# A subtraction on GpSimd cut into pieces of 256 columns, in an attention and two-layer MLP kernel

## The chip, the cores and the metric

The kernel runs on one core of a Trainium2 chip. The metric is the device time of one execution in microseconds. TensorE is called PE here, VectorE DVE, ScalarE ACT, GpSimd POOL, and SyncE SP, as in the profile.

## The reference

Three parts follow one another; the output of each is the input of the next.

1. Attention over 4 batches, 8 heads, 576 positions, head size 64. Scores are scaled by 1/8; those more than tau = 0.02 below their row's maximum are left out; softmax; product with v. The result is laid out as 2304 tokens of 512 numbers.
2. An MLP, 512 to 2048 to 512, with a rational activation between: `g = P(h) / (Q(h) + 1e-6)`, P of third and Q of second degree in h and |h|.
3. A second MLP of the same sizes with a piecewise quadratic activation: h where h >= 1, 0 where h <= -1, (h + 1)^2 / 4 between.

Inputs and outputs are float32, the four weight matrices float64. The kernel keeps close to float32 accuracy with float16 matrix products: each operand is the sum of an upper half, `hi` (its value rounded to float16), and a lower half, `lo` (what the rounding left out, again in float16). A product is made of hi x hi, hi x lo and lo x hi.

## The kernel before

**Making the halves.** ACT casts the float32 value to float16 (`hi`), then `lo = src - hi` is computed by DVE or by POOL. The function `split` (L188 to L200) does this for most operands. With no scale it is ACT's cast (L191) and POOL's subtraction (L192); with a scale and `on_vector` it is ACT's scaling (L194) and one operation on DVE (L195); with a scale and without `on_vector`, ACT scales in place (L197) and `split` calls itself with no scale, so that POOL subtracts.

**Weights.** Each layer has 8 chunks with two halves each (`x` = 0 for the first matrix, 1 for the second), a half being 128 x 1024 numbers (E = 1024). `convert` loads a half from DRAM on SP's queue (L221), turns float64 into float32 by three DVE operations on integers (L208 to L210), finds a bound (ACT's L226 and a small PE product, L170), and calls `split` without `on_vector`: so the subtraction of a weight is a POOL instruction of 1024 columns at L192, 16 times into `wc` for the first layer and 16 times into `wh` for the second. The other things that come to L192 are `gg`, the activations of the MLP steps (384 columns, 192 times), and for the first batch `qk` (576) and `v` (512). The halves go out to DRAM and are loaded again for later batches.

**Attention.** For each batch and pair of heads, q and k are loaded, split and transposed by DMA. Then come nine rows of 128 queries against 576 keys (36 rows a batch, 144 in all). Each row runs: scores on PE (L357, L358); maximum on DVE (L407 for the first batch; L410 for the others, where it also copies the scores to SBUF); two small operations (L411 on ACT, L412 on DVE); exponential on ACT (L367); the threshold applied on DVE, `e = (s >= th) * e` (L368); the cast to float16 on ACT (L376); the lower half on POOL in two instructions, the 64 columns of the last block (L377) and the other 512 columns (L378); the transpose of both halves by DMA, issued on SP's queue (L380); the product with v on PE (L393); and the normalizing on DVE, PE and ACT (L430 to L444). Three rows' `hl` and `eT` buffers exist (N_ROW = 3).

**MLP.** Tokens go through in 12 blocks of 192 for each layer, and each block in 8 steps, one for each chunk. A step makes the first product on PE (L641), the activation on ACT and DVE (L526 to L535 for the first layer, L586 to L588 for the second; L529, L530 and L588 read the product in PSUM, L528, L533, L534, L535 and L587 read SBUF alone), the halves `gg` (ACT's L191, POOL's L192), and the second product (L655). The second product of a step is issued three steps later (LAG = 3).

**Order.** The work of the first batch's attention and the first layer's weights comes first. Then run the 192 MLP steps, and beside them the second layer's weights (spread over steps 0 to 20) and the attention of the following batches (`ATTENTION`, spread over steps 18 to 147). Each group of instructions gets a due time by `at(...)`, and the planner of the language orders each engine's instructions by those times, the dependences and its own estimates. On the chip every engine runs its instructions strictly in that order; SP's queue issues almost all DMAs, in order too.

Of the kernel before, what the change touches and what calls it, by code (L numbers as in the profile page):

```python
# [12 lines left out]
ALU = mybir.AluOpType  # L13
# [23 lines left out]
def tile_attention_moe_moe2(  # L37
# [18 lines left out]
    V, A, G, T, Q = nc.vector, nc.scalar, nc.gpsimd, nc.tensor, nc.sync  # L56
    B, H, S, D = q.shape
    P = 128
# [14 lines left out]
    E = KT * CF  # L73
# [114 lines left out]
    def split(hi, lo, src, scale=None, on_vector=True):  # L188

        if scale is None:  # L190
            A.copy(hi, src)  # L191
            G.tensor_tensor(lo, src, hi, op=ALU.subtract)  # L192
        elif on_vector:
            A.activation(hi, src, AF.Copy, scale=scale)  # L194
            V.scalar_tensor_tensor(lo, src, scale, hi, op0=ALU.mult, op1=ALU.subtract)  # L195
        else:
            A.activation(src, src, AF.Copy, scale=scale)  # L197
            split(hi, lo, src)
# [14 lines left out]
    def convert(m, i, x, dst, on_vector):  # L213

        if x == 0:
            raw = rp.tile([P, KT, CF * words], raw_type, name=f"rw{m}_{i}_0", tag="rw")
            src = w_in_dram[m][:, i * CF * words : (i + 1) * CF * words].rearrange("(kt p) f -> p kt f", p=P)
        else:
            raw = rp.tile([P, NF, DM * words], raw_type, name=f"rw{m}_{i}_1", tag="rw")
            src = w_out_dram[m][i * CF : (i + 1) * CF, :].rearrange("(f p) d -> p f d", p=P)  # L220
        Q.dma_start(raw, src)  # L221
        name = f"{m}_{i}_{x}"
        src = as_float(raw.rearrange("p a b -> p (a b)"), name)
        hi, lo = dst[:, 0:E], dst[:, E : 2 * E]
        bound = small(1, "mb" + name)
        A.activation(hi, src, AF.Square, scale=2.0**-32, accum_out=bound)  # L226
        s = root("pw" + name, f_w[m][x][:, i : i + 1], everywhere("mw" + name, bound, 1), even=m == 1 and x == 1)
        split(hi, lo, src, s, on_vector)
        if m == 0 and x == 0:

            pg = ps_1.tile([P, 512], F32, name="pg" + name, tag="aux")[:, 0:CF]
            cols = hi.rearrange("p (kt f) -> p kt f", kt=KT)
            for f in range(NF):
                c = slice(f * P, (f + 1) * P)
                for kt in range(KT):
                    T.matmul(pg[:, c], cols[:, kt, c], cols[:, kt, c], start=(kt == 0), stop=(kt == KT - 1))
            V.tensor_reduce(gram[:, i : i + 1], pg, axis=AX.X, op=ALU.max)
        elif i == NCH - 1:
            f_max[m][x] = small(1, f"f_max{m}{x}", True)
            V.tensor_reduce(f_max[m][x], f_w[m][x], axis=AX.X, op=ALU.max)  # L240
# [29 lines left out]
    def prep_v(b, on_vector):  # L270
# [24 lines left out]
        for g, raw in enumerate(raws):  # L295
            n = H if g == H // hs else hs * NT
            for n0 in range(0, n, 8):
                n1 = min(n, n0 + 8)
                to = vv[:, g * hs * NT + n0 : g * hs * NT + n1]
                split(to[:, :, 0:D], to[:, :, D + 1 : 2 * D + 1], raw[:, n0:n1], s_x[b], on_vector)  # L300
        return vv

    def prep_pair(b, pr, on_vector):
# [23 lines left out]
        for x in range(2):  # L327
            split(qk[:, x, :, 0:D], qk[:, x, :, D : 2 * D], raw[:, x], s[:, x : x + 1], on_vector)
# [12 lines left out]
    M = NT * P  # L341
# [19 lines left out]
    def softmax(b, s, ab, con, nb, th, name):  # L361

        if b == 0:
            e = mp.tile([P, 2 * W], F32, name="e" + name, tag="tp", bufs=N_TEMP)[:, 0:S]
        else:
            e = ap.tile([P, S], F32, name="e" + name, tag="e", bufs=N_SC)
        A.activation(e, s, AF.Exp, bias=nb, scale=con[:, 0:1])  # L367
        V.scalar_tensor_tensor(e, s, th, e, op0=ALU.is_ge, op1=ALU.mult)  # L368
        hl = ap.tile([P, 2 * S], F16, name="hl" + name, tag="hl", bufs=N_ROW)
        if ab == 0:  # L370

            hi, whole, half, lo_w, lo_h = hl[:, 0:S], slice(0, M), slice(M, S), hl[:, S + ST :], hl[:, S : S + ST]
        else:

            hi, whole, half, lo_w, lo_h = hl[:, S:], slice(ST, S), slice(0, ST), hl[:, 0:M], hl[:, M:S]
        A.copy(hi, e)  # L376
        G.tensor_tensor(lo_h, e[:, half], hi[:, half], op=ALU.subtract)  # L377
        G.tensor_tensor(lo_w, e[:, whole], hi[:, whole], op=ALU.subtract)  # L378
        eT = ap.tile([P, C, P], F16, name="eT" + name, tag="eT", bufs=N_ROW)
        Q.dma_start_transpose(out=eT, in_=hl)  # L380
        return eT
# [13 lines left out]
    def att_rows(b, pr, g, data, pvs):  # L395

        con, qkT, kT2, vv, h = data
        name = f"{b}_{pr}_{g}"
        rows = ROWS[3 * g : 3 * g + 3]
        for r, (t, ab) in enumerate(rows):  # L400
            other = b == 0 and r % 2 == 1
            banks = ps_2.tile([P, 1024], F32, name=f"s{name}_{r}", tag="acc" if other else "s")
            scores(banks, t, ab, qkT, kT2)
            mx, nt = small(1, f"mx{name}_{r}"), small(2, f"nt{name}_{r}")
            if b == 0:
                s = banks[:, 0:S]
                V.tensor_reduce(mx, s, axis=AX.X, op=ALU.max)  # L407
            else:
                s = ap.tile([P, S], F32, name=f"sc{name}_{r}", tag="sc", bufs=N_SC)
                V.tensor_scalar(s, banks[:, 0:S], 1.0, -LARGEST, op0=ALU.mult, op1=ALU.max, accum_out=mx)  # L410
            A.activation(nt[:, 1:2], mx, AF.Identity, bias=ln_e, scale=con[:, 1:2])  # L411
            V.tensor_scalar(nt[:, 0:1], mx, con[:, 2:3], None, op0=ALU.add)  # L412
            eT = softmax(b, s, ab, con, nt[:, 1:2], nt[:, 0:1], f"{name}_{r}")
            if ab == 0:
                pv = ps_1.tile([P, 512], F32, name=f"pv{b}_{pr}_{t}", tag="ph" if b == 0 else "pv", bufs=2 if b == 0 else 1)
                pvs[t] = pv[:, 0 : 2 * (2 * D + 2)].rearrange("p (a d) -> p a d", a=2)
            if t < NT:
                weighted(pvs[t][:, ab], slice(0, P), eT, slice(0, P), vv, h + ab, ab)
            else:
                for i in range(2):  # L420
                    c = slice(i * ST, (i + 1) * ST)
                    weighted(pvs[t][:, 0], c, eT, c, vv, h + i, 0)
            if ab == 1 or t == NT:
                normalize(b, pr, t, pvs.pop(t))
# [331 lines left out]
```

## Time and profile before

| | |
|---|---|
| three runs | 1320.09, 1316.28, 1324.3 us; median 1320.09 |
| the profiled execution | 1324.86 us; its span from the first to the last instruction 1323.1 us |
| mean granted TensorE clock | 0.916 of full speed |
| busy: PE, DVE, ACT, POOL | 1056.3, 1050.1, 839.3, 515.6 us |

Engines: the busy time of each is a mean over stages that differ much, so a table by stretches stands first among the rows below. In a list of a line's instructions, a duration that is far above the median, on an engine that runs in order, is time in which the instruction was issued and could not go on. In the timeline a row is an instruction: its start, its duration, its engine and line.

### The profile page before, as it was taken

How to read it: one execution, taken by the hardware profiler on the slowest of the kernel's cores; microseconds unless marked ns; L12 is line 12 of the kernel's file. 1: busy time of each engine (PE TensorE's matmuls, PEld its weight loads, DVE VectorE, ACT ScalarE, POOL GpSimd, SP SyncE). 2: the span in 40 equal slices, each digit the busy share in tenths (PEclk: the TensorE clock that was granted, in tenths of full speed). 3: DMA queues.
4: the chain of work that ended last, by engine and by line, in shares of the span. 5: the costliest groups of instructions: out<-in, count | busy, mean ns of one | idle time of the engine just before them, and what ended most of it. 6: DMA issues, size and time to landing. Idle time of an engine off the chain costs nothing.

```text
span 1323.1 us, 31559 instructions
## 1 busy us (share of the span) xinstructions
PE 1056.3 (80%) x12498; PEld 961.1 (73%) x12498; DVE 1050.1 (79%) x2461; ACT 839.3 (63%) x1515; POOL 515.6 (39%) x541
## 2 busy tenths in 40 slices
PE   1455555677754899889888999999889998999998
PEld 1233334577743888789777888898778898999998
DVE  6777776899979999678999776779998777897421
ACT  3767764677754676667676576767765776776332
POOL 2656563344332555432145354321354453222221
PEclk9985556799976999899999999999999999999999
DMA  6778875433566666781278465922586549205100
GB/s 211 221 204 225 204 190 176 147 113 112 195 258 202 119 118 108 162 243 29 73 185 201 95 121 105 242 62 46 134 216 132 94 80 258 79 2 192 65 14 26
DMA packets 260277, 187.14 MB, mean 141 GB/s; under 512 B 220960, under 2 KB 233248, under 8 KB 251936
## 3 DMA queue, kind: packets, MB, share of 16 engines
q1 hardware_dynamic: 260128, 185.12, 54.9%
q8 instruction: 98, 1.61, 0.5%
q14 instruction: 51, 0.42, 0.1%
HBM read 106.96 MB, written 21.50 MB: 97 GB/s over the span
## 4 chain that ended last, share of the span: by engine, by line
DVE 31%; PE 26%; DMA 12%; issue 11%; ACT 8%; POOL 7%; SPq 2%; DVEq 0%; POOLq 0%; ACTq 0%
PE acc L655 12%; PE ph L641 11%; DMA eT<-hl 7%; DVE e L368 4%; POOL hl L378 3%; DVE wt L209 2%; DMA qkT<-qk 2%; DVE sc L410 2%; DMA rqk<-in_k_dram 2%; DVE t L534 2%; DVE t L535 2%; PE pv L393 2%; DVE t L533 2%; DVE t L587 2%; POOL gg L192 2%
## 5 line engine op out<-in xcount | busy, mean ns | idle before, releaser
L655 PE MATMUL acc<-gg,wc 128*128 128x192 f16 x4608 | 428.4, 248 | 12.4 <-POOL gg L192 6.3
L641 PEld LDWEIGHTS <-wc 128*128 128x128 f16 x4608 | 393.8, 100 | 47.0 <-DVE t L530 29.3
L655 PEld LDWEIGHTS <-wc 128*128 128x128 f16 x4608 | 385.6, 99 | 13.4 <-issue 11.8
L192 POOL TENSOR_TENSOR gg<-t,gg 128x384 f16<-128x384 f32 x192 | 197.9, 1031 | 476.1 <-ACT gg L191 382.3
L641 PE MATMUL ph<-xT,wc 128*128 128x192 f16 x2304 | 221.9, 255 | 34.5 <-DVE t L530 32.4
L641 PE MATMUL ph<-yT,wc 128*128 128x192 f16 x2304 | 219.5, 248 | 1.2 <-DVE t L588 0.9
L378 POOL TENSOR_TENSOR hl<-e,hl 128x512 f16<-128x512 f32 x144 | 173.5, 1205 | 0.0
L393 PE MATMUL pv<-v,eT 128*128 128x65 f16 (+1 forms) x2240 | 105.8, 206 | 67.2 <-DMA eT<-hl 58.7
L393 PEld LDWEIGHTS <-eT 128*128 128x128 f16 (+1 forms) x2240 | 94.1, 109 | 84.0 <-DMA eT<-hl 71.4
L191 ACT CAST gg<-t 128x384 f16<-128x384 f32 x192 | 97.1, 507 | 87.6 <-DVE t L588 43.8
L377 POOL TENSOR_TENSOR hl<-e,hl 128x64 f16<-128x64 f32 x144 | 62.4, 433 | 198.8 <-ACT hl L376 198.4
L357 PE MATMUL s<-qkT 128*128 128x512 f16 (+2 forms) x320 | 94.8, 326 | 45.6 <-DVE e L368 17.8
L376 ACT CAST hl<-e 128x576 f16<-128x576 f32 x144 | 96.2, 668 | 53.6 <-DVE e L368 43.7
L587 DVE SCALAR_TENSOR_TENSOR t<-t,c 128x384 f32<-128x384 f32 x96 | 71.6, 746 | 67.9 <-ACT t L586 67.8
L368 DVE SCALAR_TENSOR_TENSOR e<-sc,nt,e 128x576 f32<-128x576 f32 x108 | 97.4, 902 | 29.2 <-ACT e L367 28.9
L586 ACT ACTIVATE t<-ph,c 128x384 f32<-128x384 f32 x96 | 63.9, 666 | 56.7 <-PE ph L641 51.2
L367 ACT ACTIVATE e<-sc,nt,con 128x576 f32<-128x576 f32 x108 | 93.5, 866 | 6.6 <-POOL hl L378 0.2
L526 ACT ACTIVATE t<-ph,sc 128x384 f32<-128x384 f32 x96 | 55.1, 574 | 60.2 <-PE ph L641 59.9
L411 ACT ACTIVATE nt<-mx,ln_e,con 128x1 f32<-128x1 f32 x144 | 55.2, 384 | 55.1 <-DVE sc L410 44.7
L410 DVE TENSOR_SCALAR_CACHE_REDUCE sc<-s 128x576 f32<-128x576 f32 x108 | 80.9, 749 | 10.8 <-PE s L358 10.4
L531 ACT ACTIVATE t<-t,lc 128x384 f32<-128x384 f32 x96 | 67.9, 707 | 31.4 <-DVE t L528 31.1
L358 PE MATMUL s<-kT,qkT 128*128 128x512 f16 (+2 forms) x320 | 76.5, 324 | 2.8 <-DMA kT<-qkT 2.8
(172 smaller groups left out, 1646.2 us busy)
## 6 DMA issues: line engine op xcount, KB each, us to landing
wc<-scratch SPq DMA_DIRECT2D x56, 1024.0 KB, 6.0
rw<-in_moe_w_in_dram SPq DMA_DIRECT2D x16, 1024.0 KB, 5.5
rw<-in_moe_w_out_dram SPq DMA_DIRECT2D x16, 1024.0 KB, 5.6
scratch<-wc SPq DMA_DIRECT2D x8, 1024.0 KB, 4.3
scratch<-wh SPq DMA_DIRECT2D x16, 512.0 KB, 2.6
kT<-qkT SPq DMA_DIRECT2D x32, 144.0 KB, 2.6
rqk<-in_q_dram SPq DMA_DIRECT2D x16, 256.0 KB, 3.1
rqk<-in_k_dram SPq DMA_DIRECT2D x16, 256.0 KB, 3.0
```

The costliest lines, as they stand in the source:

```text
L191: A.copy(hi, src)
L192: G.tensor_tensor(lo, src, hi, op=ALU.subtract)
L357: T.matmul(s[rows, at : at + w], qkT[:, c, cols], k1[:, k0 : k0 + w], start=True, stop=False)
L367: A.activation(e, s, AF.Exp, bias=nb, scale=con[:, 0:1])
L368: V.scalar_tensor_tensor(e, s, th, e, op0=ALU.is_ge, op1=ALU.mult)
L376: A.copy(hi, e)
L378: G.tensor_tensor(lo_w, e[:, whole], hi[:, whole], op=ALU.subtract)
L393: T.matmul(pv[rows, 0:w], eT[:, c, cols], vv[:, h * NT + x if x < NT else H * NT + h, at : at + w], start=(n == 0), stop=(n == len(blocks) ...
L410: V.tensor_scalar(s, banks[:, 0:S], 1.0, -LARGEST, op0=ALU.mult, op1=ALU.max, accum_out=mx)
L587: V.scalar_tensor_tensor(u, u, top, u, op0=ALU.min, op1=ALU.mult)
L641: last = T.matmul(ph[:, f, :], w[:, wx, kt, f * P : (f + 1) * P], rhs, start=(n == 0), stop=(n == 3 * KT - 1))
L655: T.matmul(dst, w[:, wx, f, d * P : (d + 1) * P], gg[:, gx, f, :], start=(i == 0 and f == 0 and n == 0 and d % 2 == 0), stop=(i == NCH - 1 ...
```

## The change

Two places at which POOL makes a lower half are cut along the columns. In `split` without a scale, a source of 128 x 1024 (a weight's half) is subtracted in four instructions of 256 columns in place of one of 1024; other shapes stay one instruction. In `softmax`, the 512 columns of a row are subtracted in two instructions of 256; the one of 64 columns ahead of them stays. The pieces are written one after the other; values and buffers are the same.

```diff
         if scale is None:
             A.copy(hi, src)
-            G.tensor_tensor(lo, src, hi, op=ALU.subtract)
+
+            n = E // 4 if tuple(src.shape) == (P, E) else None
+            for p in [slice(c, c + n) for c in range(0, E, n)] if n else [slice(None)]:
+                G.tensor_tensor(lo[:, p], src[:, p], hi[:, p], op=ALU.subtract)
...
         G.tensor_tensor(lo_h, e[:, half], hi[:, half], op=ALU.subtract)
-        G.tensor_tensor(lo_w, e[:, whole], hi[:, whole], op=ALU.subtract)
+        for p in (slice(0, M // 2), slice(M // 2, M)):
+            G.tensor_tensor(lo_w[:, p], e[:, whole][:, p], hi[:, whole][:, p], op=ALU.subtract)
```

## Rows read from the trace of the kernel before

**Rows 1.** Busy time by stretches: us of the stretch, then each engine's.

```profile
0.00:240.00 240.00, 111.19 (x908) 73.29 (x909) 177.14 (x418) 149.73 (x260) 118.77 (x115) 0.72 0.75 204
240.00:420.00 180.00, 117.93 (x1204) 110.15 (x1204) 165.52 (x328) 117.68 (x196) 67.11 (x41) 0.84 0.48 166
420.00:1130.00 710.00, 640.80 (x8156) 592.47 (x8154) 595.94 (x1481) 474.21 (x888) 288.57 (x342) 0.98 0.61 136
1130.00:1323.00 193.00, 186.41 (x2236) 185.14 (x2233) 111.44 (x236) 97.67 (x175) 41.13 (x45) 0.99 0.17 59
```

**Rows 2.** The chain that ended last: by engine; by line, whole span; 0 to 240 us.

```profile
DVE 31%; PE 26%; DMA 12%; issue 11%; ACT 8%; POOL 7%; SPq 2%; DVEq 0%; POOLq 0%; ACTq 0%
...
by line: PE acc L655 11.7%; PE ph L641 11.1%; issue 10.8%; DMA eT<-hl 6.9%; DVE e L368 3.7%; POOL hl L378 3.0%; DVE wt L209 2.4%; DMA qkT<-qk 2.2%; DVE sc L410 2.0%; DMA rqk<-in_k_dram 1.9%; DVE t L534 1.8%; DVE t L535 1.8%; PE pv L393 1.8%
...
by line: issue 13.1%; DVE wt L209 6.5%; DMA eT<-hl 6.2%; POOL hl L378 5.9%; POOL wc L192 4.9%; DVE wt L210 4.4%; ACT wt L197 3.2%; DVE e L368 3.2%; DVE wt L208 2.7%; POOL hl L377 2.5%; DMA rqk<-in_k_dram 2.4%; PE pv L393 2.2%; ACT wc L191 2
```

**Rows 3.** Instructions of DVE lines: shortest/median/longest ns, first and last start us.

```profile
L535 DVE SCALAR_TENSOR_TENSOR t<-t,t x96: 537/554/2479, 247.6 to 1213.7; 128x384 f32<-128x384 f32 x96
...
L208 DVE TENSOR_SCALAR wt<-rw x32: 678/693/2607, 8.9 to 399.1; 128x1024 int32<-128x1024 int32 x32
...
L588 DVE SCALAR_TENSOR_TENSOR t<-ph,c,t x96: 597/617/619, 416.7 to 1307.8; 128x384 f32<-128x384 f32 x96
```

**Rows 4.** Timeline: the first and last waits behind an L378, then behind a weight.

```profile
45.39 1.03 DVE L323 SCALAR_TENSOR_TENSOR con<-qkf,cflag 128x1 f32<-128x1 f32 x1
...
1117.96 1.51 DVE L534 SCALAR_TENSOR_TENSOR t<-t,qc 128x384 f32<-128x384 f32 x1
...
24.76 2.61 DVE L208 TENSOR_SCALAR wt<-rw 128x1024 int32<-128x1024 int32 x1
...
409.60 2.12 POOL L192 TENSOR_TENSOR wh<-wt,wh 128x1024 f16<-128x1024 f32 x1 [1.52 <-issue]
409.83 2.50 DVE L195 SCALAR_TENSOR_TENSOR qk<-rqk,qk_s,qk 128x576 f16<-128x576 f32 x1
```

**Rows 5.** The chain in order of time: first and last piece with such a wait.

```profile
45.47 0.95 DVE con L323
...
1082.38 0.89 DVE t L587
```

**Rows 6.** Instructions of POOL's lines, and who waited for L192 (us, times).

```profile
L377 POOL TENSOR_TENSOR hl<-e,hl x144: 296/306/1282, 44.5 to 1117.3; 128x64 f16<-128x64 f32 x144
...
L378 POOL TENSOR_TENSOR hl<-e,hl x144: 1145/1156/1672, 44.8 to 1117.6; 128x512 f16<-128x512 f32 x144
...
L192 POOL TENSOR_TENSOR gg<-t,gg x192: 907/916/2884, 248.8 to 1309.1; 128x384 f16<-128x384 f32 x192
...
L192 POOL TENSOR_TENSOR wc<-wt,wc x16: 2120/2124/3099, 23.7 to 227.7; 128x1024 f16<-128x1024 f32 x16
...
L192 POOL TENSOR_TENSOR v<-rv,v x5: 1117/1117/1119, 36.1 to 40.4; 128x512 f16<-128x512 f32 x5
...
  POOL gg L192: 50.5, 19
  PE acc L655: 6.3, 8
```

**Rows 7.** Timeline from 59.9 us: POOL and DVE.

```profile
59.97 1.15 POOL L378 TENSOR_TENSOR hl<-e,hl 128x512 f16<-128x512 f32 x1
...
60.42 1.77 DVE L209 SCALAR_TENSOR_TENSOR wt<-rw,wt 128x1024 int32<-128x1024 int32 x1
...
61.08 1.28 POOL L377 TENSOR_TENSOR hl<-e,hl 128x64 f16<-128x64 f32 x1
```

**Rows 8.** Timeline from 517.3 us: two DVE instructions.

```profile
517.63 0.27 DVE L326 TENSOR_TENSOR con<-con,tlow 128x1 f32<-128x1 f32 x1
...
518.02 1.59 DVE L195 SCALAR_TENSOR_TENSOR qk<-rqk,qk_s,qk 128x576 f16<-128x576 f32 x1
```

**Rows 9.** What PE waited for, 420 to 1130 us: us, times, longest.

```profile
PE pv L393 <- DMA eT<-hl: 35.6, 40, 3.3
```

## The prediction

> **What bounds the kernel now.** I read the table of stretches first, because no single engine fills the span. Up to 240 us (attention of the first batch beside the first layer's weights) nothing is full: DVE works 177 of 240 us and POOL has its busiest time, 119 us. From 240 to 420 us (the two MLP layers beside the second layer's weights) DVE is the bound, 165.5 of 180 us. From 420 to 1130 us (MLP steps beside attention) PE and DVE share it, 641 and 596 of 710 us. After 1130 us PE is busy 186 of 193 us, and none of the cut instructions lie there [rows 1]. So the change can act on 1130 us.
>
> The chain of waits says on which engine time is lost: DVE 31%, PE 26%, DMA 12%, POOL 7%; L378, the row's 512 columns, has 3.0% of it, about 40 us, some 39 of its 144 instructions. In the first stage the weight's subtraction (wc L192) holds 4.9% of 240 us; with one of the second stage these are 7 of 32 instructions [rows 2].
>
> Next, durations by line. A DVE instruction whose operands lie all in SBUF mostly takes its usual time and sometimes far more: L535 554 ns and up to 2479, L208 693 and up to 2607. One that reads PSUM never does: L588 stays between 597 and 619 ns [rows 3]. The timeline shows what the long ones have in common: POOL was running when they were issued. At 45.39 us L323, 1 column wide, takes 1.03 us behind an L378; at 409.83 an operation on 576 columns takes 2.50 us behind a weight's 2.12, begun at 409.60 [rows 4]. Going through the whole timeline (duration less the shortest of that shape) I count 81 such waits of DVE behind an L378, 45.4 us together, and 14 behind a weight, 20.9 us; the first and last of each stand in the group. Laid over the chain, 62 of the 95 lie on it, with 39.4 of the 66.3 us: 25.5 us behind L378 (a share of 0.55) and 13.9 behind weights (0.66); the first and last are in the group [rows 5].
>
> **What a piece costs.** No POOL instruction of 256 columns is in the trace; it lies between 306 ns (64 columns) and 916 ns (384). The medians lie on a line: 1156 ns at 512 and 2124 at 1024 give 1.89 ns a column, hence 672 ns for 256, some 188 ns of it fixed. Instructions that follow one another overlap a little: five of 1117 ns begin within 4.3 us, one each 1.08 us, so 40 ns are saved [rows 6]. A row's two pieces take 2 x 672 - 40 = 1304 ns, 148 more than now; a weight's four 4 x 672 - 120 = 2568, 444 more. That is 144 x 0.148 + 32 x 0.444 = 35.5 us more POOL work. POOL is busy 516 us in all over the four stretches [rows 1], so most of it is hidden by POOL's idle time. On the chain it is not: 39 x 0.148 + 7 x 0.444 = **8.9 us**. In the second stage the weights' pieces also stand ahead of the MLP's subtraction (gg L192) in POOL's order; POOL's queue held gg up for 50.5 us, yet PE waited for gg only 6.3 us in all [rows 6], since a step's second product is issued three steps late. I cost that at nothing; without this cover it would be up to 2.2 us (0.444 and three DVE operations of 0.6) for each of 16 weights.
>
> **What DVE gets back.** Whether it gains depends on who goes first when a piece ends. At 60.42 us L209 waits behind L378; the next POOL instruction, L377, is issued at 61.08, before L378's end, and takes 1.28 us in place of 0.3: DVE went first and POOL waited [rows 7]. At 517.63 the tiny L326 waits for L377, and is through after 0.27 us, though L378 is next on POOL; the operation after it (L195, 518.02) waits behind L378 for 1.59 us in all [rows 8]. So I take it that a waiting DVE operation gets in between two pieces, and that the next piece then goes before the next DVE operation.
>
> With the ends of the pieces put into each of the 95 waits, the first wait shrinks from 45.4 to 23.7 us behind L378 and from 20.9 to 4.5 behind weights. But 52 of the 81 and 13 of the 14 come before the last piece, so pieces are left over. Following DVE's own order on from each, with its gaps: where the next operation reads PSUM or DVE idles, the left piece is hidden; where it needs SBUF alone, it waits again. These second waits come to 11.3 and 14.4 us. What is left of the gain is 10.4 and 2.0 us, and on the chain 10.4 x 0.55 + 2.0 x 0.66 = **7.0 us**.
>
> **What rows lose.** Where DVE gets in, the second piece of a row starts later by that operation: 52 of 144 rows, 33.5 us together by the operations' shortest times, 0.64 us each. Behind it wait the transpose L380 on SP's queue with the loads issued after it, and then PE: from 420 to 1130 us it waited 40 times, 35.6 us, for just that transpose [rows 9]. On the chain's 39 rows this is at most 39 x 0.36 x 0.64 = 9.0 us. But when the DVE operation that was let in is itself on the chain (62 of 95), the delay is no addition; I take 35% of 9.0, **3.2 us**, between the ends nothing and 9.0.
>
> **The sum:** 8.9 + 3.2 - 7.0 = +5.1 us. The profiled execution took 1324.86 us (1323.1 of it span), 4.8 above the median of the three runs, 1320.09; on the median the sum gives **1325 us**, +0.4%. Half a per cent, 6.6 us, is about what a measurement of this kernel can tell from no change, so this is no change with a lean to slower. Ends of the unknown terms: gain on the chain 0 to 22.7 us (21.7 x 0.55 + 16.4 x 0.66, no second wait), displaced rows 0 to 9.0. The case's own range is 1316 to 1331.
>
> **The rivals.** (a) *Faster: the leftovers are hidden.* If DVE, once let through, finds its next inputs late, the remaining pieces run in its idle time and second waits vanish. For it: DVE is idle 114 us of the third stage, and each PSUM reader covers 0.6 us of a piece [rows 1, 3]. Against it: in the second stage DVE has only 14.5 us idle, and there 11 of the 14 waits behind weights lie. Time: 8.9 - 22.7 = -13.8, **1306 us**.
>
> (b) *Slower: the row's path decides.* Second pieces come late, transposes too, PE starves, and DVE's gain lies beside it. Place: L378 to L380 to L393 of the third stage. It decides from the point at which PE waits for transposes oftener than DVE's waits shrink. For it: those 40 waits of PE; DMA has 12% of the chain. Against it: 31% for DVE. Price 8.9 + 9.0 = +17.9, **1338 us**.
>
> (c) *Slower: nothing is let in between pieces.* A POOL instruction is issued some 40 ns before its forerunner ends [rows 6], so pieces might keep what DVE waits for as one block. The blocks then grow by 35.5 on 234.5 us (144 x 1.156 + 32 x 2.124), the waits by 15%, 10 us, 5.9 on the chain: 8.9 + 5.9 = +14.8, **1335 us**. [...] Rows 7 and 8 show DVE let in, though between different lines' instructions, not between two pieces of one.
>
> (d) *It doesn't do what it says:* the weight's branch asks for a shape of 128x1024, and the 32 such instructions show that it is met [rows 6]; only the planner could put other work between pieces or order queues anew. No row shows that; the nearest measure is the runs' own spread of 8 us, so I let it move any case by some 4 us.
>
> **How the numbers follow.** The sum itself 0.37, (a) 0.29, (b) 0.20, (c) 0.14; (d) is spread over them. (a) has 0.29 although the second stage speaks against it, because second waits are counted with DVE's old gaps, and a DVE that runs ahead of its inputs idles more. That gives faster 0.29, same 0.37, slower 0.34. The range reaches from a little beyond (a) to a little beyond (b): 1304 to 1341.
>
> **What the profile of the changed kernel will show.** 288 instructions of 256 columns on L378's successor and 128 on the weights', median near 672 ns; POOL busy near 551 us plus waits. The longest L535 and L208 should fall from 2.5 us to about 1.9 or less; if they do not, (c) holds. Waits behind POOL should become more and shorter: if their sum falls from 66 to near 28 us, (a); near 54, the sum. PE's wait for eT in the third stage well above 35.6 us speaks for (b). I am wrong in the mechanism if second pieces do not lengthen where DVE was let in, and wrong in the size if POOL's fixed part is not near 188 ns.

## The result and the profile after

Six runs of each kernel gave a median of 1303.39 us (1299.4 to 1305.99) after the change and 1322.19 us (1316.28 to 1326.94) before it. The ratio is 0.9852, with an interval of 0.9827 to 0.9877: faster by 1.5%, some 19.6 us (1.48% of 1322.19; the two medians themselves differ by 18.8). The forecast was 1325 us, no change with a lean to slower; the time lies even under the low end of the range, 1304. Faster was the side with the smallest of the three chances. The granted clock is no rival: its median over the runs is 0.9145 after the change and 0.914 in 29 runs of before beside the first experiments (0.902 to 0.931), whose times show no relation to it (the correlation of the 29 times with their clocks is 0.04).

The first part of the page of the changed kernel, busy time of each engine and number of instructions (span 1300.9 us; granted clock 0.925):

```profile
PE 1053.0 (81%) x12498; PEld 959.5 (74%) x12498; DVE 1018.2 (78%) x2461; ACT 841.7 (65%) x1515; POOL 569.0 (44%) x781
```

Before, DVE was busy 1050.1 us with the same 2461 instructions. The shortest of a line are as long as before (L535 537 ns, its successor L539 534), so what fell, 31.9 us, is time in which they were issued and could not go on; 29.3 of it is waits behind the cut instructions (66.3 us before, 37.0 after). POOL has 240 instructions and 53.4 us more: 35.5 of it is the predicted work of the pieces, the rest is mostly POOL's own waiting.

The table of stretches, with the first three cut as in [rows 1]:

```profile
0.00:240.00 240.00, 112.51 (x950) 76.01 (x951) 174.77 (x428) 153.50 (x265) 148.71 (x206) 0.77 0.79 207
240.00:420.00 180.00, 124.96 (x1267) 115.62 (x1265) 160.39 (x346) 117.97 (x197) 75.31 (x84) 0.84 0.51 177
420.00:1130.00 710.00, 651.52 (x8322) 605.11 (x8320) 590.36 (x1488) 488.50 (x911) 308.41 (x451) 0.98 0.60 135
1130.00:1300.00 170.00, 164.05 (x1968) 162.81 (x1965) 92.67 (x202) 81.71 (x145) 36.57 (x40) 1.00 0.17 58
```

The number of PE's products in equal stretches tells who is ahead. Up to 420 us there were 908 + 1204 = 2112, now 2217; from 420 to 1130 us 8156, now 8322. The last stretch runs at the same pace as before (1968 in 170 us and 2236 in 193 us are both 11.6 a microsecond): it is shorter by 23 us because less is left to do when it begins. (The two profiled executions, 1324.86 and 1302.72 us, are 22 us apart, a little more than the medians.) So the gain is made in the first three stages, and the end only pays it out.

The chain of waits, by engine and by line:

```profile
PE 30%; DVE 26%; DMA 13%; issue 10%; POOL 10%; ACT 6%; SPq 2%; DVEq 0%; POOLq 0%; ACTq 0%
...
by line: PE acc L659 12.8%; PE ph L645 12.5%; issue 10.3%; DMA eT<-hl 8.2%; POOL hl L382 4.7%; DVE e L371 2.4%; DMA qkT<-qk 2.4%; POOL wc L195 2.1%; PE pv L397 2.1%; DVE t L532 1.9%; DVE t L537 1.8%; DVE t L538 1.8%; DMA rqk<-in_k_dram 1.7%
```

Against [rows 2] DVE's share fell from 31% to 26%, and POOL's rose from 7% to 10%: the row's subtraction (L382 now) from 3.0% to 4.7%, as the added work and the waiting of second pieces should make it.

Instructions of POOL's and DVE's lines (shortest/median/longest ns, first and last start), which answer to [rows 6] and [rows 3]:

```profile
L382 POOL TENSOR_TENSOR hl<-e,hl x288: 659/670/1691, 42.6 to 1097.5; 128x256 f16<-128x256 f32 x144
...
L195 POOL TENSOR_TENSOR wc<-wt,wc x64: 657/669/1697, 24.2 to 220.1; 128x256 f16<-128x256 f32 x64
L195 POOL TENSOR_TENSOR wh<-wt,wh x64: 660/673/1652, 231.8 to 402.9; 128x256 f16<-128x256 f32 x64
...
L539 DVE SCALAR_TENSOR_TENSOR t<-t,t x96: 534/550/1259, 239.0 to 1191.3; 128x384 f32<-128x384 f32 x96
...
L211 DVE TENSOR_SCALAR wt<-rw x32: 674/694/2916, 8.5 to 390.6; 128x1024 int32<-128x1024 int32 x32
```

The pieces have the predicted price (672 ns). The longest piece of a row, 1691 ns, is 1.0 us above the median, where an L378 of before was at most 0.5 above its own: pieces wait for DVE now. DVE's longest L539 fell from 2479 to 1259 ns; the longest L211 did not fall, for a reason that comes further down.

What PE waited for, 420 to 1130 us (us in total, times, longest), which answers to [rows 9]:

```profile
PE pv L397 <- DMA eT<-hl: 31.9, 31, 2.4
```

### The profile page after: what moved, and what is told of

It reads as the page before. It is cut to its first block, busy times and chain, and to the rows that moved or that the text cites. A ratio compares the mean times of both kernels' runs of the same rounds, so it can differ in the third digit from the quotient of the medians.

```text
span 1300.9 us, 31793 instructions
## 1 busy us (share of the span) xinstructions
PE 1053.0 (81%) x12498; PEld 959.5 (74%) x12498; DVE 1018.2 (78%) x2461; ACT 841.7 (65%) x1515; POOL 569.0 (44%) x781
## 4 chain that ended last, share of the span: by engine, by line
PE 30%; DVE 26%; DMA 13%; issue 10%; POOL 10%; ACT 6%; SPq 2%; DVEq 0%; POOLq 0%; ACTq 0%
PE acc L659 13%; PE ph L645 13%; DMA eT<-hl 8%; POOL hl L382 5%; DVE e L371 2%; DMA qkT<-qk 2%; POOL wc L195 2%; PE pv L397 2%; DVE t L532 2%; DVE t L537 2%; DVE t L538 2%; DMA rqk<-in_k_dram 2%; DVE t L539 1%; DVE wt L212 1%; DVE sc L414 1%
## 5 line engine op out<-in xcount | busy, mean ns | idle before, releaser
L659 PEld LDWEIGHTS <-wc 128*128 128x128 f16 x4608 | 384.0, 98 | 11.6 <-issue 10.2
L195 POOL TENSOR_TENSOR gg<-t,gg 128x384 f16<-128x384 f32 x192 | 190.5, 993 | 442.5 <-ACT gg L191 353.5
L382 POOL TENSOR_TENSOR hl<-e,hl 128x256 f16<-128x256 f32 x288 | 212.7, 759 | 0.0
L397 PE MATMUL pv<-v,eT 128*128 128x65 f16 (+1 forms) x2240 | 107.6, 207 | 75.3 <-DMA eT<-hl 74.8
L191 ACT CAST gg<-t 128x384 f16<-128x384 f32 x192 | 97.0, 508 | 83.7 <-DVE t L592 35.1
L380 POOL TENSOR_TENSOR hl<-e,hl 128x64 f16<-128x64 f32 x144 | 53.5, 371 | 189.9 <-ACT hl L379 189.4
L591 DVE SCALAR_TENSOR_TENSOR t<-t,c 128x384 f32<-128x384 f32 x96 | 64.8, 675 | 71.5 <-ACT t L590 71.2
L414 DVE TENSOR_SCALAR_CACHE_REDUCE sc<-s 128x576 f32<-128x576 f32 x108 | 80.9, 749 | 14.1 <-PE s L361 13.8
L535 ACT ACTIVATE t<-t,lc 128x384 f32<-128x384 f32 x96 | 67.8, 707 | 24.0 <-DVE t L532 23.6
```

The lines of the kernel that those rows point to most:

```text
L195: G.tensor_tensor(lo[:, p], src[:, p], hi[:, p], op=ALU.subtract)
L382: G.tensor_tensor(lo_w[:, p], e[:, whole][:, p], hi[:, whole][:, p], op=ALU.subtract)
L397: T.matmul(pv[rows, 0:w], eT[:, c, cols], vv[:, h * NT + x if x < NT else H * NT + h, at : at + w], start=(n == 0), stop=(n == len(blocks) ...
L659: T.matmul(dst, w[:, wx, f, d * P : (d + 1) * P], gg[:, gx, f, :], start=(i == 0 and f == 0 and n == 0 and d % 2 == 0), stop=(i == NCH - 1 ...
```

## The experiments

The kernel's planner chooses an order for each engine from the due times, the dependences and its own estimates, and a new instruction is a new thing for it to plan. Laid side by side, only about 80% of DVE's 2461 instructions, told apart by their names in the traces, stand in the same sequence in the two kernels; the first difference comes before DVE's 100th. So the change did two things at once, and the first four runs part them. Theory P is that the pieces themselves brought the gain (DVE gets in between), theory O that the planner's new order did.

### The four corners: order and pieces apart

The order of before was kept by cutting the instructions after the planner had finished: each is replaced in its place by its pieces, the first with all waits, the last with all signals (`cut_in_place` is told how many pieces, or their widths). The other way round, the pieces in the plan of the changed kernel were joined again.

```diff
@@ e1: at the end of before, when every engine's order stands @@
+    cut_in_place(nc, lambda tile, n: {512: 2 if tile.startswith('hl') else 1, 1024: 4}.get(n, 1))
@@ e2: the rows alone @@
+    cut_in_place(nc, lambda tile, n: 2 if n == 512 and tile.startswith('hl') else 1)
@@ e3: the weights alone @@
+    cut_in_place(nc, lambda tile, n: 4 if n == 1024 else 1)
@@ e4: at the end of the changed kernel @@
+    merge_in_place(nc, lambda tile, n: n == 256)
```

> The kernel before, with its planner's order on every engine kept as it is; afterwards each weight's subtraction is replaced in its place by four pieces and each row's 512 columns by two (the first piece keeps the waits, the last one the signal). Theory P (pieces): DVE's shorter waits give the gain whatever the order, so about 1303 us, ratio 0.985, DVE's waits behind the cut instructions near 37 us in place of 66. Theory O (order): pieces alone are worth what was forecast, +5 us, and the planner's new order gave some 24 us; then about 1327 us, ratio 1.004. In between: both take part.

> As the first, but only the rows' 512 columns are cut, weights stay one instruction. Theory P: the rows' waits fall from 45.4 to about 25 us, two thirds of all that is saved, so about 1310 us. Theory O: +3 us, about 1325.

> As the first, but only the weights are cut. Theory P: the weights' waits fall from 20.9 to about 12 us, a third of what is saved, so about 1316 us. Theory O: +2 us, about 1324.

> The changed kernel with its planner's order kept; afterwards the pieces, which stand one behind the other on POOL, are joined to the whole instructions of before. Theory P: the gain is lost, about 1322 us, DVE's waits behind these instructions back near 66 us. Theory O: the gain stays or grows, 1298 to 1303 us.

| order of | instructions | median us | ratio to before, interval |
|---|---|---|---|
| before | whole | 1321.45 | 1 |
| before | all cut (e1) | 1315.23 | 0.9955 (0.9933 to 0.9977) |
| before | rows cut (e2) | 1317.37 | 0.9978 (0.9958 to 0.9998) |
| before | weights cut (e3) | 1316.55 | 0.9971 (0.9950 to 0.9991) |
| after | whole (e4) | 1306.72 | 0.9892 (0.9862 to 0.9922) |
| after | all cut (the change) | 1303.39 | 0.9852 (0.9827 to 0.9877) |

Each ratio is to the runs of before made beside that kernel. By them the pieces bring 0.45% on the old order, 5.9 us; rows and weights alone 2.9 and 3.8, which about add up. On the new order they bring 0.4%, 5.3 us, though the intervals of those two kernels overlap a little. The order brings 1.08% with whole instructions, 14.3 us. So **about 14 us of the 19.6 are the planner's order and some 5 to 6 the pieces**. Both theories have a part, the order the larger one.

The first part of the page, of e4 and then of e1:

```profile
PE 1052.2 (81%) x12498; PEld 961.6 (74%) x12498; DVE 1033.9 (79%) x2461; ACT 842.0 (65%) x1515; POOL 511.8 (39%) x541
```

```profile
PE 1060.3 (81%) x12498; PEld 964.2 (73%) x12498; DVE 1029.3 (78%) x2461; ACT 839.4 (64%) x1515; POOL 584.2 (44%) x781
```

e4 has no piece in it, POOL is as busy as before, and yet DVE's waits are shorter. Summed over the timeline as in the prediction, DVE's waits behind whole or cut instructions were 66.3 us before, 55.7 in e4, 43.6 in e1 and 37.0 after.

Where the order gains is seen in the number of products again. Two stretches of the kernel before, of e4 and of the changed kernel:

```profile
220.00:370.00 150.00, 107.73 (x1098) 100.75 (x1096) 138.18 (x257) 100.46 (x166) 53.20 (x33) 0.89 0.42 149
...
560.00:1110.00 550.00, 494.89 (x6278) 460.60 (x6275) 457.31 (x1138) 370.30 (x691) 211.13 (x249) 0.99 0.59 133
```

```profile
220.00:370.00 150.00, 112.91 (x1174) 106.14 (x1173) 136.92 (x261) 103.77 (x168) 53.87 (x36) 0.90 0.43 154
...
560.00:1110.00 550.00, 508.98 (x6443) 477.55 (x6444) 465.89 (x1157) 378.40 (x704) 211.05 (x249) 0.97 0.59 136
```

```profile
220.00:370.00 150.00, 115.06 (x1199) 108.16 (x1197) 136.47 (x262) 104.18 (x170) 65.22 (x70) 0.89 0.43 155
...
560.00:1110.00 550.00, 507.07 (x6461) 474.46 (x6461) 462.59 (x1164) 379.75 (x708) 227.40 (x324) 0.98 0.59 138
```

e4 does nearly what the changed kernel does. By the starts of the first products in the timeline, after 24 MLP steps the next begins at 361 us in e4 and at 371 before, after 48 at 552 and 566, after 144 at 1083 and 1107: the lead grows in portions, and no single wait holds it. (These two executions, 1303.78 and 1324.86 us, are 21 us apart, the medians 15.)

### Why that order: smaller pieces, or chance

Two theories remained for the order. S: a planner that sees pieces of real size plans better, so other cuts shown to it should gain too. D: any disturbance of the plan throws the time somewhere within a band, and this one fell well. To tell them apart, kernels with whole instructions were run in other orders: the planner was shown pieces, which were joined afterwards (o1: rows; o2: weights in four; o3: weights in two; n6: gg in two; n7: all in pieces of 128), or a due time was moved a little (o4, n2, n4).

```diff
@@ o1: weights as before, the row in two, joined afterwards @@
-            n = E // 4 if tuple(src.shape) == (P, E) else None
+            n = None
@@ o2: the row as before; o3 besides with E // 2; n6 with W // 2 for gg alone; n7 with E // 8 and rows in four @@
-        for p in (slice(0, M // 2), slice(M // 2, M)):
-            G.tensor_tensor(lo_w[:, p], e[:, whole][:, p], hi[:, whole][:, p], op=ALU.subtract)
+        G.tensor_tensor(lo_w, e[:, whole], hi[:, whole], op=ALU.subtract)
@@ before with other due times: o4, n4, n2 @@
-                with at(t - 1.5):
+                with at(t - 1.4):
...
-                with at(t - 1.5):
+                with at(t - 1.6):
...
-            with at(2.4 * (2 * NCH - len(halves)) - 40):
+            with at(2.7 * (2 * NCH - len(halves)) - 40):
```

> The same instructions as the kernel before, in the order that the planner gives when it is shown the rows in two pieces and the weights whole; the pieces are joined after planning. Theory S (system): seeing pieces makes the planner's order better, so this lies between 1307 and 1321 us, or near 1307 if the rows matter. Theory D (any other order would do as well or badly): orders scatter by about a per cent about some mean, on both sides of 1315, with no relation to what was cut.

> As the one before it, but the planner is shown the weights in four pieces and the rows whole. Theory S: the rest of the gain, near 1307 us if weights matter. Theory D: anywhere from 1300 to 1330 us.

> The planner is shown the weights in two pieces in place of four, rows whole; joined after planning. Theory S: a part of what the four pieces' order gives, about 1312 us. Theory D: anywhere from 1300 to 1330 us, not between the neighbours.

> The kernel before with the due time of the later batches' attention a tenth of a step later (t - 1.4 in place of t - 1.5): the same instructions, no pieces anywhere, another order from the middle of the kernel on. Theory S: no change, 1321 us. Theory D: a change of the size of the new order's, several us up or down.

> The kernel before with the first layer's weights due a little later (2.7 in place of 2.4 per half): no pieces, the same instructions, another order from the first stage on. Theory S (the planner must see pieces): within some us of 1322. Theory D (orders scatter): off by up to 15 us, up or down.

> The kernel before with the later batches' attention due a tenth of a step earlier (t - 1.6): no pieces, another order from the middle on. Theory S: within some us of 1322. Theory D: off by up to 15 us, up or down.

> The planner is shown the MLP step's 384 columns in two pieces, rows and weights whole; joined afterwards, so the same instructions as before. Theory S, if any pieces on POOL help the planner: below 1315 us. Theory D: anywhere from 1300 to 1330 us.

> The planner is shown the same two cuts as in the change, but in pieces of 128 columns; joined afterwards, so the same instructions as before. Theory S: as good as the order of the change, near 1307 us or below. Theory D: anywhere from 1300 to 1330 us.

| whole instructions in the order of | median us | ratio, interval |
|---|---|---|
| the changed kernel (e4) | 1306.72 | 0.9892 (0.9862 to 0.9922) |
| rows shown in two (o1) | 1314.54 | 0.9939 (0.9913 to 0.9965) |
| all shown in pieces of 128 (n7) | 1320.93 | 1.0000 (0.9977 to 1.0023) |
| gg shown in two (n6) | 1321.20 | 1.0003 (0.9980 to 1.0026) |
| before | 1321 to 1322 | 1 |
| weights shown in four (o2) | 1322.58 | 0.9998 (0.9973 to 1.0022) |
| attention due 0.1 later (o4) | 1323.17 | 1.0007 (0.9988 to 1.0027) |
| weights shown in two (o3) | 1324.73 | 1.0029 (1.0007 to 1.0052) |
| first weights due later (n2) | 1327.30 | 1.0038 (1.0018 to 1.0058) |
| attention due 0.1 earlier (n4) | 1329.80 | 1.0069 (1.0042 to 1.0095) |

All ten run the very same instructions, and they lie 23 us apart. S falls: the finest pieces (n7) gain nothing, the weights' pieces (o2) nothing, halves (o3) lose. o1 gains 0.6%, and together with o2's nothing that does not make e4's 1.1%. How far an order is from that of before says nothing either: counted as above, 94% of DVE's instructions are in the same sequence in n6, 87% in o1, 72% in n7. D is what is left; with its wide band, 1300 to 1330 us, it was hardly at risk. By it the changed kernel's order, the best of ten by 8 us, was luck. Why just this one is good was not found; its gain is spread over 900 us, and none of the runs isolates one move.

### What the pieces cost and bring, on a fixed order

u1 adds every instruction of the change but hardly shortens a block: the extra pieces are 16 columns wide. f1 cuts twice as fine. g1 also cuts gg. All have the order of before.

```diff
@@ u1 @@
+    cut_in_place(nc, lambda tile, n: {'hl': {512: [496, 16]}, 'wc': {1024: [976, 16, 16, 16]}, 'wh': {1024: [976, 16, 16, 16]}, 'gg': {384: None}}.get(tile[:2], {}).get(n))
@@ f1: four in a row, eight in a weight; g1: as e1, and gg's 384 in two @@
+    cut_in_place(nc, lambda tile, n: {'hl': {512: [128, 128, 128, 128]}, 'wc': {1024: [128, 128, 128, 128, 128, 128, 128, 128]}, 'wh': {1024: [128, 128, 128, 128, 128, 128, 128, 128]}, 'gg': {384: None}}.get(tile[:2], {}).get(n))
+    cut_in_place(nc, lambda tile, n: {'hl': {512: [256, 256]}, 'wc': {1024: [256, 256, 256, 256]}, 'wh': {1024: [256, 256, 256, 256]}, 'gg': {384: [192, 192]}}.get(tile[:2], {}).get(n))
```

> Order of the kernel before kept; as many added instructions as in the change, but at the very end: a row's 512 columns become 496 and 16, a weight's 1024 become 976 and three of 16. The fixed part of each added instruction is paid (35.5 us more of POOL) and DVE's first waits stay as long as they are, near 63 us. If the fixed part counts on the chain as the prediction had it, +8.9 us, about 1330; if POOL's idle time and the steps' lead hide it, no change, 1322.

> Order of the kernel before kept; pieces of 128 columns, four for a row and eight for a weight. DVE's waits behind them fall below the 43.6 us of pieces of 256, to about 35; POOL's work grows by another 61 us. If the fixed part is hidden, about 1312 us, a little better than pieces of 256 (1315); if it counts, 1325 or more.

> Order of the kernel before kept; pieces of 256 as in the change, and the MLP step's 384 columns cut into two of 192 as well. DVE's waits behind these, 35 us, should fall to about 22, POOL's work grows by 192 x 0.148 = 28 us. If the rule of the first cuts holds (a third of the waits' reduction reaches the time), 1310 us; if the added work counts, 1318 or more.

| order of before | median us | ratio, interval | DVE's waits behind the cut lines, us |
|---|---|---|---|
| whole | 1321.5 | 1 | 66.3 |
| u1: 496 + 16, 976 + 3 x 16 | 1327.79 | 1.0047 (1.0028 to 1.0066) | 58.5 |
| e1: 256 | 1315.23 | 0.9955 (0.9933 to 0.9977) | 43.6 |
| f1: 128 | 1334.10 | 1.0096 (1.0076 to 1.0116) | 27.0 |
| g1: 256, and gg in two | 1314.08 | 0.9947 (0.9928 to 0.9966) | 42.7 |

The price of a piece is seen in the instructions of L378 in u1 (16 and 496 columns under one line) and in f1 (128):

```profile
L378 POOL TENSOR_TENSOR hl<-e,hl x288: 209/1122/2139, 44.2 to 1119.6; 128x496 f16<-128x496 f32 x144
```

```profile
L378 POOL TENSOR_TENSOR hl<-e,hl x576: 416/426/1502, 42.7 to 1125.5; 128x128 f16<-128x128 f32 x192
```

209 ns for 16 columns and 426 for 128 lie on the line of the prediction, 188 + 1.89 ns a column, which gives 218 and 430. So nearly all of a 16-column piece is the fixed part.

u1 and e1 add the same 240 instructions in the same places. e1 is 0.92% of 1321.5 faster, 12.2 us. DVE waits 14.9 us less in it, and rows are held up less as well: 66 of the 144 last pieces of a row are lengthened in u1, by 35.9 us together, and 41 in e1, by 23.2 us. If all of the 12.2 us came from DVE's waits, a microsecond of them would be worth some 0.82 us, the bare cost of the added instructions would be 6.2 + 7.8 x 0.82 = 12.6 us, and the gain of e1 22.7 x 0.82 = 18.6 us. The next two kernels don't bear these prices out: by them f1 (some 96 us more POOL work, 39.3 us less of waits) would be 2 us slower than before and g1 (63 us more work, 29.3 us less of waits, gg's with them) 2 us faster; they measured 12.7 slower and 7.0 faster. So no price of a microsecond of waiting is shown. What the two runs do show is that the added work costs time (u1, 6.2 us slower although DVE waits 7.8 us less) and that pieces short enough to let DVE in bring more than that cost (e1, 5.9 us faster).

In f1 DVE's waits fall by 39.3 us, and it is the slowest of all. Where that is given back is seen at two places. The first is the row. From the start of its first piece to the end of its last a row takes 1.97 us in the mean, 1.51 in e1, where the one instruction of before took 1.21, and PE waits longer for the transposes behind it. PE's product with v before, in e1 and in f1 (busy time and mean, then the idle time before it and what ended most of it):

```profile
L393 PE MATMUL pv<-v,eT 128*128 128x65 f16 (+1 forms) x2240 | 105.8, 206 | 67.2 <-DMA eT<-hl 58.7
```

```profile
L393 PE MATMUL pv<-v,eT 128*128 128x65 f16 (+1 forms) x2240 | 106.0, 206 | 71.1 <-DMA eT<-hl 62.6
```

```profile
L393 PE MATMUL pv<-v,eT 128*128 128x65 f16 (+1 forms) x2240 | 106.2, 206 | 91.0 <-DMA eT<-hl 81.8
```

The second is DVE's first weight operation, before, in e1 and in f1:

```profile
L208 DVE TENSOR_SCALAR wt<-rw 128x1024 int32<-128x1024 int32 x32 | 28.0, 875 | 7.4 <-POOL wh L192 3.4 <-DMA rw<-in_moe_w_out_dram 2.0 <-DMA rw<-in_moe_w_in_dram 1.4
```

```profile
L208 DVE TENSOR_SCALAR wt<-rw 128x1024 int32<-128x1024 int32 x32 | 27.8, 870 | 12.0 <-POOL wh L192 5.8 <-POOL wc L192 2.6 <-DMA rw<-in_moe_w_out_dram 1.9
```

```profile
L208 DVE TENSOR_SCALAR wt<-rw 128x1024 int32<-128x1024 int32 x32 | 31.7, 991 | 24.6 <-POOL wh L192 12.5 <-POOL wc L192 8.9 <-DMA rw<-in_moe_w_in_dram 1.6
```

DVE stands ahead of it and waits for the last piece of a weight, 21.4 us in f1 where it was 3.9 before, and the operation itself has not become shorter (991 ns in the mean for 875). So part of what was a wait inside instructions is now a wait for the data. How f1's loss divides between the two was not tried apart.

g1 is not apart from e1 (the intervals overlap nearly whole). POOL's instruction of 192 columns:

```profile
L192 POOL TENSOR_TENSOR gg<-t,gg x384: 538/549/2452, 247.9 to 1298.8; 128x192 f16<-128x192 f32 x192
```

Two of 549 ns less 40 of overlap are 1058 where one took 916: 27 us more work on POOL in all 192, for 5.7 us less of DVE's waits behind gg (35.1 in e1, 29.4 in g1; 22 had been expected).

### Who goes first between two pieces

The trace of e1 shows it. POOL's instructions, then DVE's, around two rows in the timeline (start, duration in us; two pieces with nothing of POOL between are one row, x2):

```profile
57.69 2.27 POOL L378 TENSOR_TENSOR hl<-e,hl 128x256 f16<-128x256 f32 x2
...
450.06 1.85 POOL L378 TENSOR_TENSOR hl<-e,hl 128x256 f16<-128x256 f32 x2
```

```profile
58.15 1.28 DVE L209 SCALAR_TENSOR_TENSOR wt<-rw,wt 128x1024 int32<-128x1024 int32 x1
...
450.57 0.81 DVE L368 SCALAR_TENSOR_TENSOR e<-sc,nt,e 128x576 f32<-128x576 f32 x1
```

Two pieces with nothing in the way take 1.30 us, as the prediction had it (1.304). Here they take 2.27 and 1.85, and the DVE instruction issued during the first piece takes its usual time (L209's median is 1.28, L368's 0.82): DVE went in between, and the second piece waited. In e1 this happened to 41 of the 144 second pieces of a row, 23.2 us together, and each time the trace has a DVE instruction that was issued before the first piece ended and ran first; the prediction had 52 and 33.5 us. In that trace no DVE instruction waited past more than one end of a piece; its longest L208 takes 1.76 us. The changed kernel has 32 late second pieces of a row, longer by 18.6 us together than the shortest, and ahead of each a DVE instruction ran that was issued before the first piece ended.

It also has an exception among the weights, again POOL and then DVE:

```profile
152.38 2.55 POOL L195 TENSOR_TENSOR wc<-wt,wc 128x256 f16<-128x256 f32 x4
```

```profile
152.57 2.92 DVE L211 TENSOR_SCALAR wt<-rw 128x1024 int32<-128x1024 int32 x1
```

All four pieces ran through without a gap (4 x 672 - 120 = 2568 ns), and DVE's instruction, issued during the first of them, waited for the last. It is the L211 of 2916 ns above. It is no accident of one execution: in the trace of g2 (the last kernel below, of the same order) the same instruction waits again, 2.94 us from 153.09 us on. f1 has another one: at 55.98 us an L208, the same operation on a weight, takes 2.42 us, past a row's L377 and all four pieces of 128. Why this operation was not let in there is open.

### Both gains together

The last kernel is the changed one, in its own order, with gg cut in two afterwards:

```diff
+    cut_in_place(nc, lambda tile, n: {'hl': {512: None}, 'wc': {1024: None}, 'wh': {1024: None}, 'gg': {384: [192, 192]}}.get(tile[:2], {}).get(n))
```

> The changed kernel with its planner's order kept, and the MLP step's 384 columns cut into two of 192 in their place. If waits decide, some 4 us below the changed kernel's 1303; if the added 28 us of POOL count, above it, 1306 to 1310.

1299.94 us (1294.92 to 1303.95), ratio 0.9840 (0.9814 to 0.9865). It beats the kernel before by 1.6%; against the changed kernel's 0.9852 (0.9827 to 0.9877) the intervals overlap, so whether it is better than that is not settled.

## Why the prediction was wrong

**The step that failed is (d).** The prediction said: only the planner could order queues anew, "no row shows that", and so it may move any case by some 4 us, half the spread of the runs. That spread is that of one program run again; it says nothing of another program. The order moved the time by 14 us, and ten orders of the same instructions lie from 1306.7 to 1329.8 us. With 12 us either way, half of those 23 (known only from these runs), around each case, the low end would have stood below (a)'s 1306 by enough to hold the measured time, and the chance of no change would have been smaller. The direction could not have been foreseen from these rows.

**The sum, on a fixed order, had the wrong sign too.** It said +5.1 us where e1 measured -5.9.

- *Price of a piece, 672 ns:* right (669 to 673). POOL's busy time of 551 us plus waits: right, 569.0 with 20.8 us more of waits (74.6 for 53.8 before).
- *Cost on the path, 8.9 + 3.2 = 12.1 us:* neither borne out nor refuted. u1, with the same added work, is 6.2 us slower although DVE waits 7.8 us less; what it would be without that gain no run shows. The rows' part had 52 late second pieces and 33.5 us; e1 has 41 and 23.2.
- *DVE's gain, 7.0 us:* this term was mis-sized. With the prediction's own cost of 12.1 the measured -5.9 needs a gain of 18.0 us, with u1's 6.2 alone one of 12.1. The prediction had 66 us of waits fall to 54; they fell to 43.6 in e1. Second waits were over-counted: 25.7 us of them were put on top of 28.2 us of first waits. They were laid into the old gaps of DVE, though a DVE that runs ahead may find its next inputs later. That is the mechanism of (a), and the prediction named it as the reason for (a)'s chance. L208's wait for a weight's last piece (3.9 us before, 8.4 in e1) fits it; that it makes up the difference is argued, not shown. Whether the shares of the chain, 0.55 and 0.66, were too low as well can't be told.
- *gg behind the weights' pieces at nothing:* PE waited for POOL's gg 6.3 us before, 7.0 in e1 and 4.6 in the changed kernel, so the cover held.

**The rivals.** (a), all second waits gone and -13.8 us: half right on the fixed order, 43.6 us of waits where (a) had 28 and the sum 54. Its 1306 us lies nearest to the measured time, but for another reason, by luck: most of the gain is the order's. (b), the row's path: falls for this change. Second pieces came late, less often than predicted, and PE's wait for the transposes went from 35.6 us in [rows 9] to 36.7 in e1 and 31.9 in the changed kernel, not well above. Over the whole span it did grow, from 58.7 us to 62.6 in e1 and 74.8 in the changed kernel (71.5 in e4, so by the order mostly), and the time fell all the same. In f1, the slowest, it is 81.8: with pieces of 128 (b) has a part. (c), nothing let in: falls by the timeline above and by e2 and e3, both on the faster side of 1, but for the exceptions. In e1 each of the 41 late second pieces of a row came after a DVE instruction that was issued while the first piece ran. The L211 of 2.92 us was not let in so: issued during the first of four pieces, it waited for all.

**The marks that were set.** Waits more and shorter, the longest L539 below 1.9 us (1.26), second pieces longer where DVE was let in, 288 and 128 instructions: all as said. Only L211's longest (2.92 us) was not, by its exception.

## What to carry to other kernels

Where a planner orders the instructions, an edit's own worth is only seen with the order held fast: cut or join in place after planning, and give "a new order" a price of its own, taken from several plans of the same instructions and not from repeated runs of one. Here POOL's subtraction and DVE held each other up. Smaller pieces shortened DVE's waits (66.3 us behind whole instructions, 43.6 at 256 columns, 27.0 at 128), while each piece cost its fixed part and the row ended later (1.21, 1.51 and 1.97 us from its first start to its last end): on a fixed order 256 columns (672 ns, 188 of it fixed) gained 0.45%, 128 (426 ns) lost 1%. Where a trace shows two engines in each other's way like this, find the size by trying both.

## What the runs showed that was not expected

- Ten orders of the same instructions lie between 1306.7 and 1329.8 us, 1.7% apart, with nothing in the instructions or in the share of common order that told which is good.
- Busy time of DVE is no measure of work in such a kernel: the same 2461 instructions were busy 1050.1 us before, 1018.2 in the changed kernel and 1013.4 in f1, which is slower than before by 1%.

```profile
PE 1056.5 (80%) x12498; PEld 960.8 (72%) x12498; DVE 1013.4 (76%) x2461; ACT 839.3 (63%) x1515; POOL 669.6 (50%) x1197
```

- A DVE instruction went in ahead of every late second piece of a row in e1 (41 of 41) and in the changed kernel (32 of 32), but in three traces (the changed kernel, g2, f1) one instruction, each time DVE's first operation on a weight, was kept out by four pieces in a row, 2.4 to 2.9 us.
